# Attention, a gated product and routed experts in one kernel: order of the first attention, of g's low parts and of the router's products

## The chip, the cores and the metric

One core of a Trainium2 chip runs the whole kernel as one program. The metric is the device time in microseconds from launch to end, the median of several runs. Engines are named as the profile names them: PE (matrix products), DVE (vector), ACT (scalar), POOL (GpSimd), SP (issues nearly all DMAs).

## What is computed

```python
# _attn_ref: q, k, v are (4, 8, 576, 64); heads 0-3: a window of 32 keys, heads 4-7: every fourth key of 128
scores = np.where(masks, scale * q @ k.T, -1e9)
attn = softmax(scores)
x = attn @ v                                   # 2304 tokens x 512
# _moe_ref: d_ff = 1536
x = ((x @ w_a) * (x @ w_b)) @ w_out
# _moe2_ref: 8 experts, each token goes to the one with the largest logit
logits = (x / |x|) @ (emb / |emb|).T / tau
out[mask_e] = gate * (relu(x[mask_e] @ w1[e]) @ w2[e])
```

The weights w_a, w_b and w_out come as 64-bit floating point words and are turned into 32-bit numbers on the chip.

## The kernel before

The tokens come in four batches b = 0 to 3 of 576. Every product is made of three PE passes: a number is split into a high part (an ACT copy to a shorter format) and a low part (a subtraction on DVE or POOL), and `mm3` (lines 576 to 580) multiplies high by high, high by low and low by high. That is why lines 578, 579 and 580 carry nearly all matmuls.

**First attention** (loop at line 1019, thirteen steps). The nine row tiles j of batch 0 go through a hand-written pipeline: `scores` (PE products with the mask, DVE maxima, POOL scaling, line 434), `exp` one step later (ACT, four pieces), `norm` (POOL, DVE, POOL), `trans` (PE transposes of the weights, LAG = 3 steps after the scores), `tevac` (the copy of the transposed weights to `aT`, ACT), `av` (PE, one more step later), `oevac` (ACT writes `x0h`, DVE `x0l`). In the same steps the first two weight tiles are converted (`CONV_STEPS`), the first one is split in four quarters (`SPLIT0`, low parts on POOL), and a first part of the next products is made ahead (`PRE`). The loads are issued by SP in the order `ORDER`: mask, q/k, v, conversion words and constants.

**f loop** (line 1064; `f_step`, line 593). Each batch has twelve steps f, each over a slice of 128 columns of w_a and w_b. A step has four product groups on PE, `mm(c, hf)`: c chooses w_a or w_b, hf one half of the tokens, each into a PSUM bank of its own. After both groups of a half, `g_evac` has ACT copy one product (`a`), DVE multiply it with the other (`g`), ACT write the high part `gh` (line 610) and POOL the low part `gl` (line 611). Between the groups stand: the attention of the next batch (scores of tile f, transposes and `av` of tile f-2), `ab_split` of the next weight slice (`abh` on ACT, `abl` on DVE), and two lists of small things, `extra` after the first `g_evac` and `extra2` before the last group. In b = 0 each step also converts one weight tile (`conv_steps`: ACT scales the high words, three DVE operations assemble the number) and loads the words of a later one into one of two buffers (`conv_load`); the result is stored for the later batches. `setup2` in `extra2` of step 6 normalises the expert embeddings in a chain of small DVE operations.

**x1 stage** (`x1_run`, `x1_last`, `x1_weights`, line 662). After the twelve steps of a batch, twelve steps multiply g by w_out. In b = 0 four more tiles of w_out are converted here, one at each even step, all four parts of it ahead of the split of the next half tile (`wo_split`: `woh` on ACT, `wol` on POOL in b = 0 and on DVE later).

**Router**. The rows of x1 of a batch are multiplied with the eight expert embeddings on DVE (`logit`, line 219, one operation for each row tile and expert), during the f loop of the next batch: three in each `extra2` of b = 1 and 2, six in those of b = 3. `choose`, `rank`, `place` and the `scatter` of the rows (POOL) follow in later steps of the same generator (`steps`, line 279).

**Experts**. The rest of the time, from some 570 us on, belongs to the eight experts and is not touched.

Every engine runs its instructions in the order in which the program issues them; an instruction that waits holds up what stands behind it on the same engine. SP's DMAs too are issued in program order.

Of the kernel before, what the change touches and what calls it, by code (L numbers as in the profile page):

```python
# [29 lines left out]
LOGITS = 3  # L30
# [50 lines left out]
def fused_kernel(ctx: ExitStack, tc: tile.TileContext, qk, v, wab, wout, w1, w2, emb, tau, cst, msk, out, dbg=None):  # L81
# [51 lines left out]
    def setup():  # L133
        e_sb = cv.tile([E, DM], F32, tag="esb", name="esb", bufs=1)
        t_sb = rt.tile([E, 1], F32, tag="tsb", name="tsb", bufs=1)
        nc.sync.dma_start(out=e_sb, in_=emb)
        nc.sync.dma_start(out=t_sb, in_=tau)
        return e_sb, t_sb

    def setup2(e_sb, t_sb):  # L140
        junk = cv.tile([E, DM], BF16, tag="ejunk", name="ejunk", bufs=1)
# [37 lines left out]
    class Router:  # L179
# [208 lines left out]
    class Attn:  # L388
# [102 lines left out]
    def conv_load(i):  # L491
        if i < len(conv_src):
            t = c64[i] = cv.tile([128, 2048], I32, tag="c64", name="c64")
            nc.sync.dma_start(out=t, in_=conv_src[i].bitcast(I32))
# [11 lines left out]
    def conv_steps(i):  # L506
# [7 lines left out]
        else:  # L514
            wo_raw[i - NF] = dst
        keep = wab32[i] if i < NF else wout32[i - NF]
        words = c64[i].rearrange("p (n two) -> p n two", two=2)
        lo, hi = words[:, :, 0], words[:, :, 1]
        ou = dst.bitcast(U32)
        nc.scalar.activation(out=hi.bitcast(F32), in_=hi.bitcast(F32), func=AF.Copy, scale=REBIAS)  # L520
        yield
        nc.vector.tensor_scalar(out=ou, in0=hi.bitcast(U32), scalar1=3, scalar2=None, op0=ALU.logical_shift_left)
        yield
        nc.vector.scalar_tensor_tensor(
            out=ou, in0=hi.bitcast(U32), scalar=0x80000000, in1=ou, op0=ALU.bitwise_and, op1=ALU.bitwise_or)
        yield
        nc.vector.scalar_tensor_tensor(
            out=ou, in0=lo.bitcast(U32), scalar=29, in1=ou, op0=ALU.logical_shift_right, op1=ALU.bitwise_or)
# [63 lines left out]

    def f_step(b, f, at_cur, at_mid, at_prev, extra, extra2):
# [7 lines left out]
        def g_evac(hf, between=None):  # L601
# [6 lines left out]
            if between is not None:  # L608
                between()
# [715 lines left out]
```

## Time and profile before

| | |
|---|---|
| median of 3 runs | 825.92 us (824.6 to 826.48) |
| the profiled execution | 822.89 us, its span 821.1 us, mean granted TensorE clock 0.994 |
| busy: PE, DVE, ACT, POOL | 787.6 us (96%), 495.3 (60%), 406.1 (49%), 216.7 (26%) |
| chain that ended last, by engine | PE 56%, DVE 12%, ACT 11%, DMA 7% |
| first attention | from the start to about 35 us |
| f loop and x1 of b = 0, 1, 2, 3 | from about 35, 173, 311 and 439 us |

A busy time is that of the instructions of an engine, without what it waited for. Matmuls overlap in the array, so the duration of one (0.3 us) is longer than the distance to the next one. The releaser in square brackets behind a row is what ended the idle time before it. Records of neighbouring instructions on one engine overlap by about 0.1 us. A queue name with q (SPq) is the engine's instruction queue.

### The profile page before, as it was taken

To read this page: it belongs to the slowest core of one execution; us is meant where nothing else is said; L and a number is where in the kernel's file an instruction comes from. 1 tells how busy PE (TensorE), PEld (TensorE's weight loads), DVE (VectorE), ACT (ScalarE), POOL (GpSimd) and SP (SyncE) were. 2 spreads that over 40 slices of the span, in tenths; PEclk is the share of its full clock that TensorE was granted. 3 is DMA by queue.
4 is the path that set the end of the run, shared out by engine and by line. 5 is a ranking of instruction groups with operands and counts; after the bars stand their busy time and mean duration, and the time that the engine had idled before them with its cause. 6 is when DMAs were issued, how large, how long until landed. Compare 5 with 4: busy or idle time off the path is not lost.

```text
span 821.1 us, 15985 instructions
## 1 busy us (share of the span) xinstructions
PE 787.6 (96%) x6112; PEld 726.0 (88%) x6112; DVE 495.3 (60%) x1127; ACT 406.1 (49%) x1019; POOL 216.7 (26%) x295
## 2 busy tenths in 40 slices
PE   7899898999999999999999989999999999999995
PEld 4699897789989889998889889999889999999994
DVE  4688887737665426675645874355666555656671
ACT  6866554345654225555324244354564645745651
POOL 3544335533332203333220122341110001101111
PEclk9999999999999999999999999999999999999998
DMA  9967678699443322131143222546556546656720
GB/s 316 299 168 252 212 251 260 200 337 308 148 138 91 129 86 91 58 120 53 62 162 100 78 78 90 186 162 214 186 176 197 195 121 223 183 167 201 231 76 25
DMA packets 40293, 136.17 MB, mean 166 GB/s; under 512 B 4083, under 2 KB 4339, under 8 KB 37776
## 3 DMA queue, kind: packets, MB, share of 16 engines
q1 hardware_dynamic: 37120, 125.54, 47.3%
q0 software_dynamic: 3088, 9.52, 3.0%
q8 instruction: 50, 0.82, 0.4%
q14 instruction: 35, 0.29, 0.1%
HBM read 109.67 MB, written 25.80 MB: 165 GB/s over the span
## 4 chain that ended last, share of the span: by engine, by line
PE 56%; DVE 12%; issue 12%; ACT 11%; DMA 7%; POOL 1%; POOLq 0%; DVEq 0%; ACTq 0%
DVE jl L219 6%; PE mm L578 6%; PE mm L580 5%; PE mm L579 5%; DMA out_dram<-yo,ixi 5%; PE xr L579 4%; PE xr L580 4%; ACT s L439 4%; PE xr L578 4%; ACT abh L542 3%; PE hp L580 3%; PE hp L579 3%; PE hp L578 3%; DVE g L607 2%; PE ytp L579 2%
## 5 line engine op out<-in xcount | busy, mean ns | idle before, releaser
L578 PE MATMUL mm<-x0h,abh 128*128 128x288 f32 x768 | 235.7, 307 | 2.5 <-DVE g L607 2.5
L580 PE MATMUL mm<-x0h,abl 128*128 128x288 f32 x768 | 227.0, 296 | 1.7 <-DVE abl L543 1.7
L579 PE MATMUL mm<-x0l,abh 128*128 128x288 f32 x768 | 226.6, 295 | 0.0
L578 PEld LDWEIGHTS mm<-x0h,abh 128*128 128x128 f32 x768 | 144.4, 188 | 8.7 <-DVE g L607 3.2
L580 PEld LDWEIGHTS mm<-x0h,abl 128*128 128x128 f32 x768 | 144.5, 188 | 2.7 <-DVE abl L543 2.7
L579 PEld LDWEIGHTS mm<-x0l,abh 128*128 128x128 f32 x768 | 144.7, 188 | 0.0
L611 POOL TENSOR_TENSOR gl<-g,gh 128x288 fp32r<-128x288 f32 x96 | 85.5, 890 | 197.2 <-ACT gh L610 197.2
L610 ACT ACTIVATE gh<-g 128x288 fp32r<-128x288 f32 x96 | 42.7, 445 | 181.4 <-DVE g L607 181.4
L543 DVE TENSOR_TENSOR wl<-raw,wh 128x1024 fp32r<-128x1024 f32 x60 | 73.1, 1223 | 53.4 <-ACT wh L542 53.3
L543 DVE TENSOR_TENSOR abl<-abr,abh 128x1024 fp32r<-128x1024 f32 x47 | 57.8, 1230 | 77.4 <-ACT abh L542 77.4
L954 POOL DMA_INDIRECT out_dram<-yo,ixi x23 | 26.2, 1140 | 205.7 <-ACT yo L953 159.1
L543 DVE TENSOR_TENSOR wol<-wor,woh 128x512 fp32r<-128x512 f32 x48 | 38.5, 801 | 61.7 <-ACT woh L542 59.8
L542 ACT ACTIVATE woh<-wor 128x512 fp32r<-128x512 f32 x60 | 37.6, 629 | 74.3 <-PE xr L580 52.2
L578 PE MATMUL hp<-xTh,wh 128*128 128x352 f32 (+6 forms) x224 | 68.9, 308 | 0.0
L579 PE MATMUL hp<-xTl,wh 128*128 128x352 f32 (+6 forms) x224 | 67.7, 302 | 0.0
L580 PE MATMUL hp<-xTh,wl 128*128 128x352 f32 (+6 forms) x224 | 67.6, 302 | 0.0
L542 ACT ACTIVATE wh<-raw 128x1024 fp32r<-128x1024 f32 x64 | 67.0, 1053 | 0.0
L579 PE MATMUL xr<-wol,gh 128*128 128x512 f32 x156 | 61.4, 394 | 2.9 <-POOL wol L543 2.5
L578 PE MATMUL xr<-woh,gh 128*128 128x512 f32 x156 | 61.4, 393 | 2.3 <-ACT woh L542 1.7
L580 PE MATMUL xr<-woh,gl 128*128 128x512 f32 x156 | 60.8, 390 | 0.0
L607 DVE TENSOR_TENSOR g<-a,mm 128x288 f32<-128x288 f32 x96 | 42.6, 444 | 23.5 <-PE mm L580 19.2
L542 ACT ACTIVATE abh<-abr 128x1024 fp32r<-128x1024 f32 (+1 forms) x51 | 51.1, 1002 | 0.0
(213 smaller groups left out, 1665.7 us busy)
## 6 DMA issues: line engine op xcount, KB each, us to landing
raw<-in_w_dram SPq DMA_DIRECT2D x64, 512.0 KB, 4.5
abr<-wab SPq DMA_DIRECT2D x36, 512.0 KB, 3.9
c<-in_wab_dram SPq DMA_DIRECT2D x12, 1024.0 KB, 6.1
wor<-wout SPq DMA_DIRECT2D x24, 512.0 KB, 3.4
qkt<-in_qk_dram SPq DMA_DIRECT2D x12, 832.0 KB, 8.4
vt<-in_v_dram SPq DMA_DIRECT2D x12, 576.0 KB, 7.8
xs<-rows SPq DMA_DIRECT2D x8, 781.5 KB, 15.9
wab<-abr SPq DMA_DIRECT2D x12, 512.0 KB, 6.8
```

The lines of the kernel that those rows point to most:

```text
L219: nc.vector.scalar_tensor_tensor(out=jl, in0=rbox[0][:, self.t0 + t, :DM], scalar=1.0, in1=ebox[e // E1][:, e % E1, :], op0=ALU.mult, op1= ...
L439: nc.scalar.activation(out=self.s[:, pr, :], in_=self.src[pr], func=AF.Exp, scale=0.125, bias=self.least[:, pr:pr + 1], accum_out=self.sm[ ...
L542: nc.scalar.activation(out=hi, in_=raw, func=AF.Copy)
L543: (eng or nc.vector).tensor_tensor(out=lo, in0=raw, in1=hi.bitcast(F32), op=ALU.subtract)
L578: nc.tensor.matmul(out=out_, lhsT=lh, rhs=rh, start=first, stop=False)
L579: nc.tensor.matmul(out=out_, lhsT=lh, rhs=rl, start=False, stop=False)
L580: nc.tensor.matmul(out=out_, lhsT=ll, rhs=rh, start=False, stop=last)
L607: nc.vector.tensor_tensor(out=g, in0=a, in1=acc[1, hf], op=ALU.mult)
L610: nc.scalar.activation(out=g_hl[0][:, f, t], in_=g, func=AF.Copy)
L611: nc.gpsimd.tensor_tensor(out=g_hl[1][:, f, t], in0=g, in1=g_hl[0][:, f, t].bitcast(F32), op=ALU.subtract)
L954: nc.gpsimd.indirect_dma_start(out=out, out_offset=bass.IndirectOffsetOnAxis(ap=self.ixi[e][:m, t:t + 1], axis=0), in_=yo[:m, :], in_offse ...
```

## The change

In the first attention the transposes are issued ahead of the `av` products and LAG is 2, so that the loop has twelve steps. The load order is another: the second q/k group and a v group stand ahead of the words, the constants `c_sb` come in step 3. The conversion of the first two tiles and the quarter splits stand in later steps. The copies `aT` of the first five tiles go to DVE. In the f loop gh and gl of each half are put in a list and issued by `g_lows`: that of the second half in the next step, after the split, transposes and exp, that of the first half right after its g. The router's steps are called from `extra` and `extra2`, with two and one products in turn (b = 1 and 2) or two and two (b = 3); the x1 stage calls them twice in each step. In the x1 stage of b = 0 a conversion is spread over an even and an odd step, one word load is issued in two halves, one of them ahead into a buffer of its own, and the low parts `wol` are made by DVE. The embedding tiles use buffers of other tags.

```diff
-LOGITS = 3
-CONV_STEPS = (0, 0, 1, 1, 1, 1, 1, 1, 1, 1, 1, 0, 0, 0, 0, 0, 0, 0)
+CONV_STEPS = (0, 0, 0, 0, 1, 1, 1, 1, 0, 1, 1, 1)
 CONV1 = 3
-SPLIT0 = (6, 7, 8, 9)
-PRE = (10, 11)
-ORDER = (0, 1, 3, 1, 2, 2, 4)
-LAG = 3
+SPLIT0 = (8, 8, 9, 9)
+PRE = (9, 10)
+TEVAC_DVE = 5
+ORDER = (0, 1, 1, 2, 3, 2)
+LAG = 2
...
     def setup():
-        e_sb = cv.tile([E, DM], F32, tag="esb", name="esb", bufs=1)
+        e_sb = mp.tile([E, DM], F32, tag="wol", name="esb")
...
         def steps(self, per):
-            n = E * self.nt
-            for i in range(0, n, per):
-                for k in range(i, min(i + per, n)):
-                    self.logit(k)
+            n, i = E * self.nt, 0
+            while i < n:
+                k = min(n, i + per[0])
+                per = per[1:] + per[:1]
+                for i in range(i, k):
+                    self.logit(i)
+                i = k
                 yield
             self.choose()
-            yield
-            yield
+            for _ in range(3):
+                yield
             self.rank()
...
         def tevac(self):
             self.aT = at.tile([96, 4, 128], F32, tag="aT", name="aT")
-            nc.scalar.activation(out=self.aT, in_=self.tp, func=AF.Copy)
+            if self.early and self.j < TEVAC_DVE:
+                nc.vector.tensor_copy(out=self.aT, in_=self.tp)
+            else:
+                nc.scalar.activation(out=self.aT, in_=self.tp, func=AF.Copy)
...
+    def conv_ahead(i):
+        c64[i] = [cv.tile([128, 1024], I32, tag="c64x", name="c64x", bufs=1)]
+        nc.sync.dma_start(out=c64[i][0], in_=conv_src[i].bitcast(I32)[:, :1024])
...
-            split(wo_raw[n // 2][:, w], *hl, eng=nc.gpsimd if n < NF else nc.vector)
+            split(wo_raw[n // 2][:, w], *hl, eng=nc.vector)
...
+    g_low = []
+
+    def g_lows():
+        while g_low:
+            g_low.pop(0)()
+
...
             nc.vector.tensor_tensor(out=g, in0=a, in1=acc[1, hf], op=ALU.mult)
-            if between is not None:
-                between()
-            nc.scalar.activation(out=g_hl[0][:, f, t], in_=g, func=AF.Copy)
-            nc.gpsimd.tensor_tensor(out=g_hl[1][:, f, t], in0=g, in1=g_hl[0][:, f, t].bitcast(F32), op=ALU.subtract)
+
+            def low():
+                nc.scalar.activation(out=g_hl[0][:, f, t], in_=g, func=AF.Copy)
+                nc.gpsimd.tensor_tensor(out=g_hl[1][:, f, t], in0=g, in1=g_hl[0][:, f, t].bitcast(F32), op=ALU.subtract)
+
+            g_low.append(low)
...
             at_mid.norm()
+        g_lows()
         mm(1, 0)
         g_evac(0)
+        g_lows()
         conv(cg, 2)
...
         if b == 0:
             conv_store()
+            if i == 0:
+                conv_ahead(NF + 4)
             if i % 2 == 0:
-                conv(conv_steps(NF + 2 + i // 2))
-                conv_load(NF + 4 + i // 2)
+                x1_conv[:] = [conv_steps(NF + 2 + i // 2)]
+                conv(x1_conv[0], 2)
+            else:
+                conv(x1_conv[0], 1)
...
             wo_split(n + 1)
+        if b == 0:
+            conv(x1_conv[0], 1)
+            if i % 2:
+                conv_load(NF + 4 + i // 2)
...
+                nc.sync.dma_start(out=c_sb, in_=cst)
+            if i in (5, 9):
+                load_v()
...
-            if LAG + 1 <= i:
-                gr[i - LAG - 1].av()
             if LAG <= i < NJ + LAG:
                 gr[i - LAG].trans()
                 gr[i - LAG].tevac()
+            if LAG + 1 <= i:
+                gr[i - LAG - 1].av()
...
-                steps = router.steps(6 if last else LOGITS)
+                steps = router.steps((2, 2) if last else (2, 1))
...
                 elif router is not None:
+                    extra.append(lambda: next(steps, None))
                     extra2.append(lambda: next(steps, None))
...
-                x1_run(b, 10 if b == 0 else None, lambda i: next(steps, None))
+                x1_run(b, 10 if b == 0 else None, lambda i: [next(steps, None) for _ in range(2)])
```

## Rows read from the trace of the kernel before

**Rows 1.** Windows of 10 us: busy us (and instructions) per engine, granted clock, DMA.
```profile
20.00:30.00 10.00, 7.03 (x116) 4.85 (x113) 6.86 (x20) 9.10 (x44) 6.66 (x13) 1.00 1.00 354
160.00:170.00 10.00, 10.00 (x46) 8.28 (x45) 3.29 (x3) 2.85 (x4) 5.72 (x5) 1.00 0.68 230
460.00:470.00 10.00, 8.75 (x64) 8.19 (x63) 8.30 (x20) 2.63 (x6) 2.39 (x3) 1.00 0.31 102
```

**Rows 2.** Timeline of DVE, f loop of b = 3 (start us, us, instruction, idle before).
```profile
442.40 0.46 DVE L607 TENSOR_TENSOR g<-a,mm 128x288 f32<-128x288 f32 x1 [0.46 <-PE mm L580]
...
474.37 1.22 DVE L543 TENSOR_TENSOR abl<-abr,abh 128x1024 fp32r<-128x1024 f32 x1 [1.46 <-ACT abh L542]
...
512.88 0.45 DVE L607 TENSOR_TENSOR g<-a,mm 128x288 f32<-128x288 f32 x1
...
519.24 0.46 DVE L607 TENSOR_TENSOR g<-a,mm 128x288 f32<-128x288 f32 x1 [2.70 <-PE mm L580]
```

**Rows 3.** Timeline of ACT at three places: step 7 and x1 of b = 0; b = 3.
```profile
96.73 0.45 ACT L610 ACTIVATE gh<-g 128x288 fp32r<-128x288 f32 x1 [6.68 <-DVE g L607]
...
170.93 2.64 ACT L698 ACTIVATE rows<-xr 128x512 f32<-128x512 f32 x4 [1.76 <-PE xr L580]
...
472.95 0.44 ACT L610 ACTIVATE gh<-g 128x288 fp32r<-128x288 f32 x1 [4.48 <-DVE g L607]
```

**Rows 4.** Timeline of PE: first attention, steps 6 to 8 of b = 0, x1.
```profile
19.16 0.56 PE L413 MATMUL sc<-qkt 64*64 64x96 f32 x16 [1.72 <-DMA qkt<-in_qk_dram]
...
34.41 0.69 PE L465 MATMUL av<-aT,vt 96*64 96x64 f32 x16
...
81.82 0.34 PE L407 MATMUL sc<-mask_bf,id_bf 128*128 128x192 bf16 x2
...
90.29 0.34 PE L407 MATMUL sc<-mask_bf,id_bf 128*128 128x192 bf16 x2
...
92.74 0.60 PE L452 MATMUL atp<-ident,s 128*96 128x128 f32 x4
...
98.72 0.69 PE L465 MATMUL av<-aT,vt 96*64 96x64 f32 x16 [2.19 <-ACT aT L456]
...
101.48 0.54 PE L407 MATMUL sc<-mask_bf,id_bf 128*128 128x192 bf16 x2
...
104.97 0.60 PE L452 MATMUL atp<-ident,s 128*96 128x128 f32 x4
...
133.06 0.40 PE L578 MATMUL xr<-woh,gh 128*128 128x512 f32 x1
```

**Rows 5.** Waits of PE, 174 to 262 us (b = 1): total us, times, longest.
```profile
PE av L465 <- ACT aT L456: 1.5, 4, 0.9
```

**Rows 6.** Groups by line: x1 of b = 0, its f loop, b = 3 (busy us, mean ns).
```profile
L543 POOL TENSOR_TENSOR wol<-wor,woh 128x512 fp32r<-128x512 f32 x12 | 18.8, 1575 | 14.5 <-ACT woh L542 14.4
L527 DVE SCALAR_TENSOR_TENSOR wor<-c,wor 128x1024 uint32<-128x1024 uint32 x6 | 11.2, 1870 | 0.1
L520 ACT ACTIVATE c<-c 128x1024 f32<-128x1024 f32 x5 | 5.7, 1131 | 11.8 <-DMA c<-in_wout_dram 11.8
...
L527 DVE SCALAR_TENSOR_TENSOR abr<-c,abr 128x1024 uint32<-128x1024 uint32 x10 | 12.1, 1212 | 0.0
...
L611 POOL TENSOR_TENSOR gl<-g,gh 128x288 fp32r<-128x288 f32 x23 | 18.5, 805 | 73.7 <-ACT gh L610 73.7
L219 DVE SCALAR_TENSOR_TENSOR jl<-rows,en_a 128x512 bf16<-128x512 f32 x20 | 15.5, 777 | 0.6
```

**Rows 7.** Timeline of DVE, steps 6 (`setup2`) and 10 of b = 0.
```profile
91.90 0.67 DVE L143 SCALAR_TENSOR_TENSOR ejunk<-esb 8x512 bf16<-8x512 f32 x1
...
97.76 0.60 DVE L426 TENSOR_REDUCE amx<-sc 128x2 f32<-128x192 f32 x2
...
129.52 0.44 DVE L607 TENSOR_TENSOR g<-a,mm 128x288 f32<-128x288 f32 x1
```

**Rows 8.** The page's DMA issues: KB each, median us to landing.
```profile
c<-in_wout_dram SPq DMA_DIRECT2D x6, 1024.0 KB, 6.3
```

More of the change, by code (lines that the diff above doesn't have):

```diff
@@ L140, in setup2 @@
     def setup2(e_sb, t_sb):
-        junk = cv.tile([E, DM], BF16, tag="ejunk", name="ejunk", bufs=1)
+        junk = rt.tile([128, DM], BF16, tag="jl", name="ejunk", bufs=1)[:E, :]
         ss = rt.tile([E, 1], F32, tag="ess", name="ess", bufs=1)
@@ L492, in conv_load @@
         if i < len(conv_src):
-            t = c64[i] = cv.tile([128, 2048], I32, tag="c64", name="c64")
-            nc.sync.dma_start(out=t, in_=conv_src[i].bitcast(I32))
+            c64[i] = c64.get(i, []) + [cv.tile([128, 2048], I32, tag="c64", name="c64")]
+            w = 1024 * (len(c64[i]) - 1)
+            nc.sync.dma_start(out=c64[i][-1][:, :2048 - w], in_=conv_src[i].bitcast(I32)[:, w:])
+    def conv_ahead(i):
+        c64[i] = [cv.tile([128, 1024], I32, tag="c64x", name="c64x", bufs=1)]
+        nc.sync.dma_start(out=c64[i][0], in_=conv_src[i].bitcast(I32)[:, :1024])
     conv_kept = []
@@ L516, in conv_steps @@
         keep = wab32[i] if i < NF else wout32[i - NF]
[L517 to L520, printed above, removed]
+        parts, c = [], 0
+        for t in c64.pop(i):
+            n = min(t.shape[1] // 2, 1024 - c)
+            words = t[:, :2 * n].rearrange("p (n two) -> p n two", two=2)
+            parts.append((words[:, :, 0].bitcast(U32), words[:, :, 1].bitcast(U32), dst.bitcast(U32)[:, c:c + n]))
+            c += n
+        for lo, hi, ou in parts:
+            nc.scalar.activation(out=hi.bitcast(F32), in_=hi.bitcast(F32), func=AF.Copy, scale=REBIAS)
         yield
-        nc.vector.tensor_scalar(out=ou, in0=hi.bitcast(U32), scalar1=3, scalar2=None, op0=ALU.logical_shift_left)
+        for lo, hi, ou in parts:
+            nc.vector.tensor_scalar(out=ou, in0=hi, scalar1=3, scalar2=None, op0=ALU.logical_shift_left)
         yield
-        nc.vector.scalar_tensor_tensor(
-            out=ou, in0=hi.bitcast(U32), scalar=0x80000000, in1=ou, op0=ALU.bitwise_and, op1=ALU.bitwise_or)
+        for lo, hi, ou in parts:
+            nc.vector.scalar_tensor_tensor(out=ou, in0=hi, scalar=0x80000000, in1=ou, op0=ALU.bitwise_and, op1=ALU.bitwise_or)
         yield
-        nc.vector.scalar_tensor_tensor(
-            out=ou, in0=lo.bitcast(U32), scalar=29, in1=ou, op0=ALU.logical_shift_right, op1=ALU.bitwise_or)
+        for lo, hi, ou in parts:
+            nc.vector.scalar_tensor_tensor(out=ou, in0=lo, scalar=29, in1=ou, op0=ALU.logical_shift_right, op1=ALU.bitwise_or)
         conv_kept.append((keep, dst))
@@ L599, in mm, with g_evac @@
                 ab_mm(n, acc, c, hf, k)
-        def g_evac(hf, between=None):
+        def g_evac(hf):
             a = ap.tile([128, HALF], F32, tag="a", name="a")
@@ L689, in x1_run @@
             x1_weights(b, i, NF)
+            if i == 0:
+                g_lows()
             if i == rows_at:
@@ L711, in x1_last @@
                 x1_weights(b, j, 2 * NF)
+                if j == 0:
+                    g_lows()
                 hook(j)
@@ L1040, in fused_kernel @@
             conv(early_conv, CONV_STEPS[i])
-            if i in SPLIT0:
-                ab_split_part(0, SPLIT0.index(i))
+            for q in range(4):
+                if SPLIT0[q] == i:
+                    ab_split_part(0, q)
             if i in PRE:
```

3 lines of the change are left out of this document (1 added, 2 removed).

## The prediction

> **What bounds the kernel now.** I read the 10 us windows first. TensorE (PE) is the bound wherever it is unhindered: between 160 and 170 us it runs 46 matmuls, so one takes 0.217 us. Three stretches of another kind stand beside it [rows 1]: the first attention (20 to 30 us), where PE is busy 7.03 of 10 us, ACT 9.10 and DMA all of the time; the f loop of b=3 (460 to 470 us), where PE has 8.75 and DVE 8.30 with DMA at 0.31; and, further down, the x1 stage of b=0. The gain can come from such stretches alone, so I next asked each what PE waits for. In b=3 the first g of the batch starts at 442.40, the last but one pair stands at 512.88 and 519.24 [rows 2]. The last pair is a step that only PE bounds: 6.36 us. Eleven of them are 69.96 us, and 442.40 to 519.24 is 76.84. So 6.9 us are lost there. The engine that shows why is ACT: it sits 4.48 us before gh, released by DVE's g [rows 3]. DVE works off six router products between the two g of a step, the g of the second half waits behind them, gh waits for that g, and because ACT runs in order the next split (abh) waits behind gh; abl on DVE in turn waits for abh [rows 2, 3]. The same link is seen in b=0: ACT waits 6.68 us for g and so comes late to the aT copy, and PE's av products wait 2.19 us [rows 3, 4]; and in b=1 the waits of av on aT make 1.5 us [rows 5] (the same row, 1.5 us, stands for b=2).
>
> **The change part by part.** Its own time is that of the profiled execution, 822.89 us (span 821.1 plus 1.8 around it); the median of the runs is 825.92, 3.0 higher. I sum savings and take them off the median.
>
> (1) g's low part (gh on ACT, gl on POOL) of the second half is issued one step later, behind the next abh, aT and exp; that of the first half stays right behind its g. Nothing is added: as many instructions, in another order. What is now queued behind gh on ACT is only a of the next first half, and gl's reader is the x1 stage, up to 11 steps away. So the link "g to next abh and aT" is cut.
>
> (2) b=3: four products a step instead of six, two on either side of the third product group, in eight steps instead of five and a bit. DVE per step then: 4 x (0.78 for the product + 0.08 read, an estimate from the pitch) + 1.23 for abl + 2 x 0.46 for g = 5.6 us [rows 2, 6], under PE's 6.36. Before: 6 x 0.86 + 1.23 + 0.92 = 7.3, and the wait for abh on top. The choice and rank of tokens move later (f=8 and 9 instead of 6 and 8), and the four row scatters on POOL follow in f=10 and 11, no later than the last stood before; the rank's few matmuls stay. Of the 6.9 us I keep 0.4 for those: **6.5** (5.5 to 6.9).
>
> (3) b=1 and b=2: still three products a step, but two before and one after av, and aT no longer behind gh. The waits of rows 5 go, twice 1.5: **2.9** (2.0 to 3.2). Choosing in f=11 of b=1 now precedes the last g; PE needs that bank only after three further row tiles of x1, 9 x 0.217 = 1.95 us on, so I cost it at nothing; without that cover it costs the choice, seven small DVE operations at some 0.2 us (4.2 us for 21 in rows 7, see (4)): 1.5.
>
> (4) b=0, step 7. The chain of 21 small DVE operations for the embedding norm starts at 91.90, and DVE reaches the next maxima at 97.76 [rows 7]; less the g (0.45) and the conversion (1.21, rows 6) between, the chain is 4.2 us. PE's score products start at 81.82, 90.29 and 101.48: 8.47 for the step before, 11.19 for this one, so 2.7 us lost. [...] With the link cut aT is early. What is late next is the score bank: the next scores need this step's exp, exp needs the maxima, and DVE starts those only at 97.76. They take 0.60; POOL's scaling and exp's four pieces have no row here, I put them at 1.5 (1.0 to 2.1). That gives 99.9 instead of 101.48, 1.6 gained (1.0 to 2.1), and with a wait that short I take it that the clock stays: 1.04 more. **2.7** (1.0 to 3.8, the upper end if DVE, no longer chained through ACT, is ahead when the chain begins).
>
> (5) x1 of b=0. The first product starts at 133.06, and the first evacuation, at 170.93, waits for the last product of its row tile [rows 3, 4]. Unhindered that is 11 steps of 12 matmuls plus 3 more and a tail of 0.3: 135 x 0.217 + 0.3 = 29.6 us. It took 37.9, so 8.3 are lost. ACT waits 11.8 us there for the loaded words, and POOL's low parts take 1.58 each [rows 6]. The change splits the four conversions over even and odd steps, puts half of one load ahead, and moves the 12 low parts to DVE. That adds DVE 0.7 each (half as wide as abl, whose 1.23 is in rows 2; bounds 0.6 and 1.2), two per 5.2 us pair, and takes it from POOL. The last conversion operation took 1.87 mean here and 1.21 in the f loop [rows 6]; if POOL's absence brings it back, a pair needs 3.5 + 1.4 = 4.9 us of DVE, just under PE's 5.2, with waits of up to 1 us left at each odd step. Walking through by these prices I get 1.3 us if the words arrive as before. But the word load behind the first wait is issued when DVE has finished the conversion two tiles before, and DVE there is late through the link that (1) cuts: step 10 ends on PE at about 133.06 - 6.36 = 126.7, its last g starts at 129.52 [rows 4, 7], 2.8 later; the load itself takes 6.3 [rows 8]. So the first pair comes 2 to 3 us sooner. **3.2** (0.5 to 5.5).
>
> (6) The first attention. Loads are reordered so that the second q/k group comes before the converted words; the lag falls from 3 to 2, so the loop has 12 steps for 13, and transposes go ahead of the av products. The seventh tile's scores start at 19.16 on the third q/k load and the last av at 34.41 [rows 4]: 15.25 us, six steps, 2.54 each. As many bytes stand ahead of that load as before (but for the small constants), so 19 us stays; from there five steps remain. That would give 2.5. Against it: ACT is the pace (9.10 of 10), it keeps its exp, copies, one word scaling and now all four quarter splits in two steps; only the aT copies of five tiles go to DVE, most of them before 19 us, where the load hides them. Also the second conversion ends after the loop, and the split of f=1 waits for it. At the worst nothing is gained, at the best the five steps also run 0.2 us faster each, 3.5: **2.0** (0 to 3.5).
>
> Moving the embedding tiles to other buffers and c_sb to a later place: they wait for nothing that is near; nothing.
>
> Sum 6.5 + 2.9 + 2.7 + 3.2 + 2.0 = 17.3; 825.92 - 17.3 = **808.6** (a profiled span near 804).
>
> [...] POOL's gl takes 0.81 us in b=3 [rows 6], and now the second half's gl runs beside abl. [...]
>
> **The rivals.**
> (A) As forecast, 808.6.
> (B) The conversion sets b=0's pace: terms 4 to 6 are used up by word loads that land late. For it: DMA is full in the attention [rows 1], and the conversion of the second tile now ends later there, with the load of the fourth behind it. Against: a load has 6.3 us in an 8.47 us step. Left are 6.5 + 2.9: 816.5.
> [...]
> (D) The new attention opens a PE wait like the 2.19 us of rows 4 (the early products need the first quarter splits, which come two steps later), and the clock falls: 1.04 to 1.7 us, 810. Before, a wait at 19.16 left the clock at full. [...]
> (E) Slower: two word buffers. A word tile is held about 9.5 us (estimate: a step of 8.47 and 1 more, from its scaling at a step's start to the last operation after its end), two steps are 16.9; so a load above 7.4 us stretches each step by half the excess. At 6.3 it doesn't; at 9.4, which the denser start would have to bring, 1.0 x 14 steps = 14 us are lost on top of terms 4 to 6: 831. It decides from 7.4 on, and outweighs 9.4 us of sure gain from about 8.8.
>
> **How the numbers follow.** A 0.66, B 0.13, C 0.10, D 0.07, E 0.04. A's own ends are 816.9 (9.0 in all) and 803.0 (22.9) if all terms are low or high together, which is not likely. The range 803.5 to 815.5 holds A, C and D and leaves out B and E (0.17). A measurement of this kernel can tell about 0.2% (1.7 us). All but E lie far below it; allowing for an error in a term I have not seen: faster 0.93, same 0.03, slower 0.04.
>
> **What would show it.** Right: g pitch of 6.36 to 6.4 in all of b=3 and no ACT idle before abh; av waits on aT gone in b=1 and b=2; scores of steps 7 and 8 of b=0 under 10 us apart, clock 1.00; 46 matmuls per 10 us in more of x1; the last av before 33 us. Wrong: a DVE busy share above 0.95 in b=3 (C), ACT waiting on words in the f loop (B, E), a granted clock under 1 in the attention (D).

## The result, and the profile after

The changed kernel takes 816.9 us (median of 4 runs, 814.9 to 819.4) beside 826.2 us of the kernel before (4 runs): a ratio of 0.990, 95% interval 0.987 to 0.993. It is faster by 9.3 us, not by 17.3: the forecast was 808.6, and the time lies 1.4 us above the upper end of its range, 815.5. The profiled execution's span went from 821.1 to 813.1 us, its mean granted clock from 0.994 to 0.988.

To see where the time went I cut both spans at the same instructions. The third column is the kernel of the first experiment below (old first attention, all the rest changed); the last is the change that the forecast's terms gave to the stage.

| stage, us | before | after | old attention | forecast |
|---|---|---|---|---|
| start to first scores of the f loop | 35.29 | 37.55 | 35.38 | -2.0 |
| first to third scores | 12.88 | 14.25 | 12.86 | 0 |
| third to seventh scores | 33.92 | 33.91 | 33.92 | 0 |
| seventh to ninth scores (step 7) | 19.87 | 20.57 | 18.78 | -1.7 |
| ninth scores to x1 of b=0 | 31.10 | 32.18 | 31.72 | -1.0 |
| x1 of b=0 to its first evacuation | 37.87 | 35.47 | 36.28 | -3.2 |
| to the first scores of b=2 (b=1) | 138.58 | 136.75 | 136.77 | -1.45 |
| to the first g of b=3 (b=2) | 132.89 | 130.03 | 130.04 | -1.45 |
| to the last g but one pair (b=3) | 76.84 | 70.18 | 70.19 | -6.5 |
| the rest, mostly experts | 301.86 | 302.21 | 302.06 | 0 |

Term (4), 2.7, has two places in this table: 1.66 in step 7, and 1.04 behind the ninth scores. b=1 to b=3 gave 11.4 us, more than the 9.4 that were forecast. b=0 as a whole became longer: 170.9 us before, 173.9 after.

Windows of 10 us after (columns as in [rows 1]):
```profile
20.00:30.00 10.00, 6.15 (x107) 4.07 (x99) 8.42 (x23) 7.33 (x37) 3.96 (x10) 1.00 0.78 237
30.00:40.00 10.00, 9.24 (x102) 7.73 (x102) 4.19 (x12) 6.37 (x19) 4.54 (x7) 0.83 0.62 214
...
100.00:110.00 10.00, 7.10 (x60) 6.00 (x59) 8.45 (x20) 4.77 (x16) 3.25 (x5) 0.70 0.48 156
...
460.00:470.00 10.00, 10.00 (x78) 10.00 (x77) 8.77 (x21) 4.52 (x8) 2.84 (x3) 1.00 0.27 98
```
The last row is the success: in b=3 PE is busy all the time (8.75 before). The first is the failure: between 20 and 30 us PE is busy less than before (6.15 for 7.03), ACT too (7.33 for 9.10), and DMA is at 0.78 instead of 1.00; then, at 30 to 40 and 100 to 110, the granted clock is down (0.83 and 0.70, where the kernel before had 1.00 and 0.83).

DVE, POOL and ACT in b=3 (timelines: start us, us, instruction, idle before):
```profile
440.71 0.46 DVE L629 TENSOR_TENSOR g<-a,mm 128x288 f32<-128x288 f32 x1 [0.46 <-PE mm L596]
441.08 0.69 DVE L219 SCALAR_TENSOR_TENSOR jl<-rows,en_a 128x512 bf16<-128x512 f32 x1
...
441.81 1.27 DVE L219 SCALAR_TENSOR_TENSOR jl<-rows,en_a 128x512 bf16<-128x512 f32 x1
...
510.89 0.46 DVE L629 TENSOR_TENSOR g<-a,mm 128x288 f32<-128x288 f32 x1 [2.70 <-PE mm L596]
```
```profile
441.73 0.80 POOL L633 TENSOR_TENSOR gl<-g,gh 128x288 fp32r<-128x288 f32 x1 [19.75 <-ACT gh L632]
445.48 1.24 POOL L633 TENSOR_TENSOR gl<-g,gh 128x288 fp32r<-128x288 f32 x1 [2.95 <-ACT gh L632]
```
```profile
456.39 1.06 ACT L558 ACTIVATE abh<-abr 128x1024 fp32r<-128x1024 f32 x1 [0.99 <-PE mm L595]
...
460.28 0.45 ACT L632 ACTIVATE gh<-g 128x288 fp32r<-128x288 f32 x1 [1.70 <-DVE g L629]
```
From the first row to the g at 510.89 it is 70.18 us, eleven steps of 6.38. What ends ACT's idle ahead of abh is now PE giving back the buffer (nine times in b=3, 1.2 us at most), not gh's wait for g (4.48 in [rows 3]). DVE and POOL run beside one another twice in a step: a product beside gl takes 1.27 us instead of 0.69, and a gl beside abl 1.24 instead of 0.80. With DVE at 8.77 and PE at 10.00 of 10 us this costs nothing here.

### The profile page after: what moved, and what is told of

Same layout as the page of the kernel before. It is cut to its first block, busy times and chain, and to the rows that moved or that the text cites. A ratio compares the mean times of both kernels' runs of the same rounds, so it can differ in the third digit from the quotient of the medians.

```text
span 813.1 us, 16000 instructions
## 1 busy us (share of the span) xinstructions
PE 787.5 (97%) x6112; PEld 729.0 (90%) x6112; DVE 519.6 (64%) x1147; ACT 411.6 (51%) x1015; POOL 218.8 (27%) x283
## 4 chain that ended last, share of the span: by engine, by line
PE 73%; DMA 8%; issue 7%; DVE 5%; ACT 3%; POOL 1%; SPq 0%; POOLq 0%; DVEq 0%; ACTq 0%
PE mm L594 11%; PE mm L596 10%; PE mm L595 10%; DMA out_dram<-yo,ixi 5%; PE xr L595 4%; PE xr L594 4%; PE xr L596 4%; PE hp L595 3%; PE hp L596 3%; PE hp L594 3%; PE av L471 2%; PE ytp L595 2%; PE ytp L596 2%; PE ytp L594 2%; PE atp L455 2%
## 5 line engine op out<-in xcount | busy, mean ns | idle before, releaser
L633 POOL TENSOR_TENSOR gl<-g,gh 128x288 fp32r<-128x288 f32 x96 | 95.1, 996 | 114.0 <-ACT gh L632 114.0
L559 DVE TENSOR_TENSOR wol<-wor,woh 128x512 fp32r<-128x512 f32 x60 | 46.3, 772 | 67.6 <-ACT woh L558 63.1
L558 ACT ACTIVATE woh<-wor 128x512 fp32r<-128x512 f32 x60 | 37.8, 630 | 78.5 <-PE xr L596 56.7
L632 ACT ACTIVATE gh<-g 128x288 fp32r<-128x288 f32 x96 | 42.4, 442 | 65.8 <-DVE g L629 65.8
L437 POOL TENSOR_SCALAR least<-amx 128x4 f32<-128x4 f32 x36 | 23.4, 650 | 152.4 <-DVE amx L434 100.6
```

The costliest lines, as they stand in the source:

```text
L437: nc.gpsimd.tensor_scalar(out=self.least, in0=mx, scalar1=0.125, scalar2=None, op0=ALU.mult)
L558: nc.scalar.activation(out=hi, in_=raw, func=AF.Copy)
L559: (eng or nc.vector).tensor_tensor(out=lo, in0=raw, in1=hi.bitcast(F32), op=ALU.subtract)
L632: nc.scalar.activation(out=g_hl[0][:, f, t], in_=g, func=AF.Copy)
L633: nc.gpsimd.tensor_tensor(out=g_hl[1][:, f, t], in0=g, in1=g_hl[0][:, f, t].bitcast(F32), op=ALU.subtract)
```

## What went wrong in the first attention

**Undo that part alone.** Theory: the new attention is a loss, not a gain of 2.0.
```diff
-CONV_STEPS = (0, 0, 0, 0, 1, 1, 1, 1, 0, 1, 1, 1)
-SPLIT0 = (8, 8, 9, 9); PRE = (9, 10); TEVAC_DVE = 5; ORDER = (0, 1, 1, 2, 3, 2); LAG = 2
+CONV_STEPS = (0, 0, 1, 1, 1, 1, 1, 1, 1, 1, 1, 0, 0)
+SPLIT0 = (6, 7, 8, 9); PRE = (10, 11); TEVAC_DVE = 0; ORDER = (0, 1, 3, 1, 2, 2, 4); LAG = 3
 # and av ahead of trans, c_sb ahead of the loop, the second v group one step later
```


> The changed kernel with the first attention of the kernel before (lag 3, av ahead of the transposes, old load order, old places of the conversion, all aT copies on ACT); all else as changed. Theory A: the new first attention itself loses time: the scores of step f=0 came 2.3 us later than before and those of f=2 3.6 us later. With the old one the f=0 scores stand at 35.0 and those of f=2 at 48.2 us again, and the whole gains 3.6 against the changed kernel: span 809.5, about 813. Rival B: the word loads of the f loop set the pace of b=0 anyway, and the x1 stage starts no earlier than 138 us: within 1 us of the changed kernel.

Measured: 810.1 us (809.7 to 810.9), ratio 0.982 (0.978 to 0.985). That is 6.7 us under the whole change and even under the 813 of the theory; the table's third column shows that b=0 lost less afterwards, too. So the new first attention costs 6.7 us (7.2 by the two ratios), and the rest of the change alone gains 14.8, where the other terms of the forecast sum to 15.3.

**Why.** The waits of PE from the start to 45 us (total us, times, longest), after, and then with the old attention:
```profile
PE atp L455 <- POOL s L450: 6.6, 8, 1.9
```
```profile
PE sc L410 <- ACT s L442: 2.3, 2, 1.2
PE av L471 <- ACT aT L462: 2.0, 2, 1.0
PE sc L416 <- DMA qkt<-in_qk_dram: 1.5, 2, 1.0
```
The transposes of the softmax weights wait for POOL's product s in eight steps. One such step on PE, DVE and POOL, kernel after (timelines as above):
```profile
25.52 0.56 PE L416 MATMUL sc<-qkt 64*64 64x96 f32 x16
27.27 0.64 PE L455 MATMUL atp<-ident,s 128*96 128x128 f32 x4 [1.20 <-POOL s L450]
...
30.76 0.64 PE L455 MATMUL atp<-ident,s 128*96 128x128 f32 x4 [1.91 <-POOL s L450]
```
```profile
23.29 1.58 DVE L541 SCALAR_TENSOR_TENSOR abr<-c,abr 128x1024 uint32<-128x1024 uint32 x1
24.79 0.61 DVE L429 TENSOR_REDUCE amx<-sc 128x2 f32<-128x192 f32 x2
26.13 0.18 DVE L449 RECIPROCAL asm<-asm 128x4 f32<-128x4 f32 x1 [0.73 <-POOL asm L448]
```
```profile
25.56 0.23 POOL L437 TENSOR_SCALAR least<-amx 128x4 f32<-128x4 f32 x1 [1.77 <-DVE amx L429]
25.87 0.23 POOL L448 TENSOR_SCALAR asm<-asm 128x4 f32<-128x4 f32 x1
26.39 0.83 POOL L450 TENSOR_TENSOR s<-s,asm 128x384 f32<-128x384 f32 x1 [0.30 <-DVE asm L449]
```
Read from the end: the transposes at 27.27 wait for s, which ends at 27.22; s for the reciprocal; the reciprocal for POOL's asm; asm, which belongs to an older tile, stands on POOL behind `least` of the newer one; `least` waits for the maxima, and those stand on DVE behind a conversion operation of 1.58 us. With a lag of two the transposes of a tile come one step after its s was issued, so this whole queue lies between one step's scores and the next step's transposes, and the next scores stand on PE behind those. This step takes 3.5 us (27.27 to 30.76) where [rows 4] gave 2.54. With a lag of three a further step lies between. The seventh tile's scores and the last av of the kernel after:
```profile
19.55 0.56 PE L416 MATMUL sc<-qkt 64*64 64x96 f32 x16
...
36.66 0.69 PE L471 MATMUL av<-aT,vt 96*64 96x64 f32 x16
```
The first came when it was forecast (19 us); the five steps from there took 17.1 us, 3.42 each, partly at a granted clock of 0.50 (from 32.3 to 35.7 us). The other traces agree: in all six kernels with a lag of two PE waits 5.5 to 8.8 us for s, and these five steps take 17.1 to 18.2 us. In the fourteen with a lag of three there is no such wait but one of 1.4, and the six steps take 15.3 to 17.0 us, except in two (18.9 and 21.1).

**Which part.** Six more kernels mix the two attentions; all else is as changed. "Loop" is the lag, the transposes ahead of the products and the copies on DVE; "places" are the loads, the conversion steps, the quarter splits and the early products.

| loop | places | first, third scores at | time, us |
|---|---|---|---|
| old | old | 35.4, 48.2 | 810.1 |
| new, but lag 3 | old | 38.1, 51.0 | 811.1 (810.4 to 814.4) |
| new | old | 41.6, 54.7 | 818.2 (817.4 to 819.1) |
| old | old, new loads | 42.4, 55.3 | 815.3 (814.5 to 818.6) |
| old | new | 41.4, 55.9 | 820.1 (819.0 to 822.1) |
| new, but lag 3 | new | 37.1, 51.8 | 814.0 (813.3 to 816.5) |
| new | new, old loads | 39.1, 53.9 | 817.6 (817.1 to 817.9) |
| new | new (the change) | 37.6, 51.8 | 816.9 (814.9 to 819.4) |

Their edits are the lines of the diff above, taken singly. In the order of the rows two to seven:

> The kernel with the old first attention (810.14), with only the transposes put ahead of the products and the five aT copies on VectorE; the lag stays three, loads and places as before. Theory N (the lag of two closes the loop of one step): TensorE waits under 1 us for GpSimd's product, the first scores of b=0 start at 34.5 to 36, the time is 809 to 811. Theory V (the order, or the copies on VectorE ahead of the reciprocals, slow it whatever the lag): the first scores start at 37 us or later, the time is 812 to 818.

> The kernel with the old first attention (810.14) with only its loop changed: lag of two, transposes ahead of the products, five aT copies on VectorE; loads, conversion steps, quarter splits and early products stay where they were before. Theory N (the loop of one step costs the attention, the moved conversion and splits cost the two steps after it): TensorE waits 4 us or more for GpSimd's product, the first scores of b=0 start at 36.5 to 37.5, the first to the third scores take 12.9 us as in the old attention (14.3 in the changed kernel), the time is 811 to 813. Theory P (the moved conversion and splits make both losses): the first scores start at 35.5 or sooner, one step fewer even gives 34, the time is 808.5 to 810.5.

> The kernel with the old first attention (810.14), with only the loads in their new order (second q/k group ahead of the converted words, the constants in the loop, v one step sooner); the conversion keeps its steps, from the third on. Theory L (the later words stop VectorE and ScalarE, whose conversion steps now stand ahead of their data): ScalarE waits 2 us or more for the words in the attention, the first scores start at 37 or later, the time is 812 to 818. Theory P (the late conversion and the splits crowded into two steps cost, not the loads): the first scores within 1 us of 35.4, the time is 809.5 to 811.

> The opposite: the loop of the first attention as before (lag of three, products ahead of the transposes, aT on ScalarE), with the new order of the loads and the new places of the conversion, the quarter splits and the early products. Theory N: no wait for GpSimd's product, the first scores of b=0 start at 35.3 to 36.3, but the first to the third scores take 14 us or more since the second conversion ends 7 us later, the time is 811.5 to 813.5. Theory P: the first scores start at 37 or later, the time is 814 to 817. If neither loss is here (35.5 and 12.9), the loss comes only from both together, 810.

> The changed kernel with the lag of the first attention set back from two steps to three (13 steps again); the transposes stay ahead of the products, the loads, the copies on VectorE and the split places stay as changed. Theory N (the loop of one step): with a lag of two, a tile's aT copy, the next reciprocal, GpSimd's product s and the next transposes follow each other inside every step, and TensorE waits for s 6.6 us in all; with a lag of three the product has a step of slack, so that wait falls under 1.5 us, the first scores of b=0 start near 36 us (37.55 in the changed kernel, 35.29 before), and the time is 812 to 815. Theory L (the loads): the place of the loads and of the second conversion sets the end, the first scores stay at 37.5 or later, the third set of scores at 51.8 or later, and the time is 816 to 819.

> The changed kernel with the loads of the first attention in their order of before (the converted words ahead of the second q/k group, the small constants ahead of the loop, the second v group at the seventh step); its loop with a lag of two stays. Theory N (the loop of one step): TensorE's wait for GpSimd's product stays at 5 us or more, the first scores of b=0 start at 37 us or later, the time is 815 to 819. Theory L (the loads): the second conversion ends near 34 us again (40.9 in the changed kernel), the first scores start near 35.5, the third set near 48.5, and the time is 810 to 812.

What follows. The lag of two costs 7.0 us in the old places (818.2 against 811.1) and 2.8 in the new ones (816.9 against 814.0; there the ranges overlap, and the two profiled executions, 814.9 and 816.5, stand the other way round), and with it PE's wait for s comes and goes:
```profile
PE atp L455 <- POOL s L450: 8.8, 8, 2.1
```
```profile
PE atp L455 <- POOL s L450: 1.4, 1, 1.4
```
(the new loop in the old places with a lag of two, then of three; waits of PE to 55 us). Transposes ahead and copies on DVE cost 1.0 us at most, which can't be told from nothing. The new order of the loads costs 5.2 us by itself: the words come later, ACT waits 5.46 us for them with exp queued behind, and PE waits 6.01 us for exp (ACT, then PE, in that kernel; its profiled execution was the slowest of the four, 818.6 us):
```profile
16.00 1.10 ACT L535 ACTIVATE c<-c 128x1024 f32<-128x1024 f32 x1 [5.46 <-DMA c<-in_wab_dram]
```
```profile
18.12 0.64 PE L410 MATMUL sc<-mask_bf,id_bf 128*128 128x192 bf16 x2 [6.01 <-ACT s L442]
```
The later conversion steps of the change avoid that wait, but then the second conversion ends at 41.0 us instead of before the loop, and f=1's abh and the word load behind it come late (ACT, kernel after):
```profile
41.02 1.06 ACT L558 ACTIVATE abh<-abr 128x1024 fp32r<-128x1024 f32 x1 [2.11 <-DVE abr L544]
...
48.21 1.15 ACT L535 ACTIVATE c<-c 128x1024 f32<-128x1024 f32 x1 [3.08 <-DMA c<-in_wab_dram]
```
This is the 1.4 us between first and third scores: 14.3 to 14.8 in the four kernels with new places, 12.9 to 13.2 in the four with old ones. Along the rows one, two, six and eight of the table the 6.7 us are 1.0 for the order and the copies, 2.9 for the new places and 2.8 for the lag. Of my prices for the halves (1 to 3 us each) none held: each half alone costs 8 to 10 us, both together 6.7. They don't add up. Each alone lets the clock fall further than both together (0.83 in this stretch); that this makes the difference is likely, not shown. Windows of the new loop alone, then of the new places alone:
```profile
30.00:40.00 10.00, 7.11 (x64) 5.95 (x66) 4.77 (x11) 4.37 (x19) 5.44 (x6) 0.60 0.76 242
```
```profile
30.00:40.00 10.00, 7.42 (x51) 5.42 (x51) 2.73 (x11) 4.80 (x19) 4.69 (x8) 0.66 0.62 217
```
Why the new places alone cost most of all stays open; one wait that the change does not have is PE's of 1.1 us for POOL's part of a quarter split.

A mark comes from one execution, and it wanders: the nine kernels here with the very same old attention began their first scores at 35.1 to 40.4 us. In rows two, four and six the profiled execution was the slowest of its four by 2 to 3 us, in row eight it was the fastest. And the kernel before, run beside each group of kernels, had medians from 824.6 to 826.2. The verdicts above go by the times, and differences of 1 or 2 us between two marks are not read.

## b=3: two cuts, one would do

> The changed kernel, but the low parts of both halves are issued right after their g in every batch; the router's products stay spread. Theory A: b=1 and b=2 owe their gain to the deferral and lose it (4 to 5 us), and in b=3 the chain g, gh, abh, abl, g, four products makes 6.7 us a step for PE's 6.36, another 2 to 3 us; b=0 gains 1 to 2: 822. Rival B: the spread alone does it, in all batches: within 2 us of the changed kernel.

> The changed kernel with the router's products where they were before (three, in b=3 six, in one place ahead of the last product group, one call in each x1 step); the low parts stay deferred. Theory A: in b=3 DVE has 7.3 us of work in a step of 6.36, so the first steps run at 7.3: some 5 us of that batch's 6.7 are lost again, b=1 and b=2 keep their gain: 822. Rival B: the wait of the split behind gh was the whole cause, the deferral alone brings 6.36 us steps: within 1 us of the changed kernel.


```diff
         g_evac(1)
+        g_lows()          # first kernel: no deferral, products spread as changed
...
-                steps = router.steps((2, 2) if last else (2, 1))   # second: deferral, products as before
+                steps = router.steps((6,) if last else (3,))   # and called once a step
```
Measured: 820.6 and 818.8 us (ratios 0.995 and 0.993), but little of what they lose to the change lies in b=3: their f loops begin 1.7 and 1.3 us later, and the first takes 2.2 us more in x1 of b=0. By stage, b=3 takes 70.83 without the deferral and 70.44 without the spreading, beside 70.18 with both and 76.84 with neither. So either cut alone opens the loop: without the six products in a row g is early enough for gh, and with gh deferred a late g holds up nobody (without the spreading gh still waits up to 3.7 us for g, but abh for PE alone). My shares in b=3 (2 to 3 us for the deferral, some 5 for the spreading) were wrong: taking one away cost 0.65 or 0.26, since the other does its work. In b=1 and b=2 the deferral is worth about 0.8 us each (137.5 and 130.95 without it), the spreading next to nothing (136.8 and 130.2 without it); without the deferral 1.1 and 1.9 us of the gain stay.

## b=0: step 7 and x1

**Step 7.** The kernel after, timelines of ACT and of PE:
```profile
103.63 1.06 ACT L558 ACTIVATE abh<-abr 128x1024 fp32r<-128x1024 f32 x1 [5.45 <-DVE abr L544]
```
```profile
102.51 0.40 PE L594 MATMUL mm<-x0h,abh 128*128 128x288 f32 x1 [1.75 <-DVE g L629]
105.70 0.64 PE L410 MATMUL sc<-mask_bf,id_bf 128*128 128x192 bf16 x2 [1.15 <-ACT s L442]
```
The deferral moved gh behind abh and exp. But in b=0 abh waits for the last conversion operation (line 544), which stands on DVE behind that same g. The link that I called cut is there a second time. PE waits 1.75 and 1.15 us, and the clock is at 0.50 from 104 to 110.7 us.

> The first attention of before and everything else as changed, but in b=0 g's second low part is issued at once. It stands against the kernel with the old first attention, 810.14. Theory A (as in the forecast, the deferral pays in b=0 too): the seventh to the ninth scores lie 20 us apart instead of 18.78, x1 begins over 1 us later, 811.5 to 812.5. Theory B (abh waits in b=0 for the last operation of the conversion, which stands behind that same g, so the deferral frees nothing there): every mark within 0.4 us, the time 809.7 to 810.6, and the 2.3 us that the same edit cost the changed kernel was the spread of the new first attention.

> The first attention of before and everything else as changed, but the chain of 21 small VectorE operations for the embedding norm, in one step of b=0 so far, is given out over six steps. It stands against the kernel with the old first attention, 810.14. Theory A (the chain is the cause of the late step): the seventh to the ninth scores take 16.9 to 17.3 us instead of 18.78, the time is 807.5 to 808.7. Theory B (VectorE has no room): it holds 7.8 us of work in a step of 8.47, 0.7 more a step fills it, six steps become 0.2 to 0.4 us longer, and the time is 809.5 to 811.


```diff
         g_evac(1)
+        if b == 0:
+            g_lows()                                   # first kernel
...
-                if b == 0 and f == 6:                  # second kernel
-                    extra2.append(lambda: es.append(setup2(*es[0])))
+                if b == 0 and f == 4:
+                    es_steps = setup2(*es[0])          # now a generator, some operations a step
+                if b == 0 and 4 <= f < 10:
+                    extra2.append(lambda: next(es_steps, None))
```
The same undoing in the changed kernel with its new attention had given 819.2 us, with the first scores at 40.7:

> The changed kernel, but in b=0 alone the low parts of the second half are issued right after their g, as before. Theory A: in b=0 the next split waits on ACT for the last conversion operation, which stands behind g on DVE, so that the deferral cut nothing there; it only put gh between exp and the next a, and two gl side by side beside the conversion. Then the distance of the scores of f=6 and f=8 falls from 20.6 us to 19.9 or less and x1 starts some 1.8 us earlier: 815. Rival B: the deferral does shorten the way to the conversion of the last tiles, and x1 loses 1 to 2 us without it: 818.

Measured: 812.9 us without the deferral in b=0 (810.1 with it). 1.2 of the 2.8 us lie in the start of that execution, 0.4 in step 7, 1.1 in x1. So it frees little where I looked for it. The time is far from theory B's (809.7 to 810.6) and 0.4 above theory A's, but the place that A named is not it: the seventh to the ninth scores take 19.2 us, not 20. With the chain spread the seventh to the ninth scores take 16.96 us, two steps of 8.48: the chain was the whole loss of step 7, and DVE has room for it. Yet the time is 811.8, not lower: x1 took 37.8 instead of 36.3, and the stage ahead of it 0.6 more.

**x1.** With the old attention, PE and ACT:
```profile
138.50 0.50 PE L594 MATMUL xr<-woh,gh 128*128 128x512 f32 x1 [1.67 <-ACT woh L558]
```
```profile
130.10 1.15 ACT L535 ACTIVATE c<-c 128x1024 f32<-128x1024 f32 x1 [3.15 <-DMA c<-in_wout_dram]
136.80 1.14 ACT L535 ACTIVATE c<-c 128x1024 f32<-128x1024 f32 x1 [3.09 <-DMA c<-in_wout_dram]
143.40 1.14 ACT L535 ACTIVATE c<-c 128x1024 f32<-128x1024 f32 x1 [4.09 <-DMA c<-in_wout_dram]
```
woh stands on ACT behind a scaling whose words have not landed; after that wait the clock is at 0.83 between 140 and 150 us. Two theories: the order on ACT and DVE, or the words, which come every 6.6 us, where PE needs a new pair every 5.44 us (24 matmuls, 0.68 us for three).

> The kernel with the old first attention (810.14), and in x1 of b=0 the split of the next weight tile is issued ahead of the scaling of the loaded words in the even steps (it was behind it). Theory S (ScalarE's order: woh stands behind words that have not landed, TensorE waits 1.7 us at the second step and its clock falls to half): no wait of TensorE for woh, clock 1.00 in x1, first x1 product to first evacuation 32 to 33.5 us instead of 36.2, the time is 806.5 to 808. Theory W (the words themselves set the pace of x1): the wait moves to the next tile of the converted weights, the stage stays at 35.5 us or more, the time is 809.5 to 811.

> As the run before it, and the embedding-norm chain is given out over six steps. Alone the chain's 1.8 us were given back in x1. Theory S: with the split ahead, x1 no longer takes them, the time is 1.3 to 2 us under the run before it, 805 to 806.5. Theory W: x1 ends when the words have come, so nothing is added: within 0.5 us of the run before it.

> The kernel with the old first attention (810.14), and in x1 of b=0 every split of the next weight tile is issued ahead of the conversion steps, even and odd. Theory S2 (the order on ScalarE and VectorE sets x1): TensorE waits under 0.7 us for woh and wol in all, the clock stays at 1.00, first x1 product to first evacuation 31.5 to 33 us instead of 36.2, the time is 805.5 to 807.5. Theory W (the words set x1's end): the scaling of the words still comes every 6.6 us, the waits move to the tiles of the next pair, 35 us or more, the time is 809 to 811.

> As the run before it, and the embedding-norm chain is given out over six steps. Theory S2: x1 starts 1.3 us sooner and keeps at least half of that at its end: 804 to 806.5, at least 0.6 under the run before it. Theory W: x1's end stands where the words put it, the time is within 0.5 us of the run before it.

> The kernel with the old first attention, splits ahead and the chain spread (808.69), and in b=0 the half tile of words that is loaded ahead is that of the fourth output weight tile, a load issued two f steps before x1, instead of that of the fifth. Theory W (the words set x1's end): the scaling of the fourth tile, 7.4 us behind the third's so far, comes 4.5 to 6 us behind it, the wait of TensorE for wol at 149.0 (1.1 us) goes or moves to the fifth tile, x1 takes 34 to 35.2 us instead of 35.8, the time is 807 to 808.5. Theory E (the engines' order sets it): x1 within 0.3 us of 35.8, the time within 0.5 us of 808.7.


```diff
         if b == 0:
             conv_store()
+            if i + 1 < n_i:
+                wo_split(n + 1)              # split_all; split_first only for even i
...
+            if f == 9:                       # words_ahead: in f_step, instead of conv_ahead(NF + 4) in x1
+                conv_ahead(NF + 3)
             conv_load(n + 4)
```

| with the old attention | x1, us | time, us |
|---|---|---|
| alone | 36.3 | 810.1 (809.7 to 810.9) |
| even splits ahead | 35.9 | 810.4 (809.5 to 812.3) |
| even splits ahead, chain spread | 37.4 | 810.1 (809.3 to 812.8) |
| all splits ahead | 36.0 | 810.4 (808.1 to 812.8) |
| all splits ahead, chain spread | 35.8 | 808.7 (807.3 to 809.8) |
| the same, words of the fourth tile ahead | 35.3 | 812.9 (811.4 to 816.1) |

With all splits ahead the wait for woh is gone and the clock holds (ACT and a window of that kernel):
```profile
131.91 1.17 ACT L535 ACTIVATE c<-c 128x1024 f32<-128x1024 f32 x1 [2.38 <-DMA c<-in_wout_dram]
139.55 1.13 ACT L535 ACTIVATE c<-c 128x1024 f32<-128x1024 f32 x1 [3.37 <-DMA c<-in_wout_dram]
147.02 1.11 ACT L535 ACTIVATE c<-c 128x1024 f32<-128x1024 f32 x1 [3.48 <-DMA c<-in_wout_dram]
```
```profile
140.00:150.00 10.00, 8.74 (x36) 6.61 (x36) 6.60 (x8) 4.42 (x7) 0.99 (x1) 1.00 0.98 341
```
But x1 is no shorter: the words now come every 7.6 and 7.5 us, PE's waits have moved to wol (3.0 us in three), and all its waits in x1 grew from 3.0 to 3.7 us. So the order theory falls, and the words are the likelier bound: a load starts when DVE has freed one of two buffers (the kernel after has SP waiting 19.3 us for it there, in four waits), and DMA is at 0.98. The run meant to settle it met neither forecast. With half a tile's words ahead ACT waits for none after 142 us, but the loads behind are later: ACT waits 5.38 us for words just ahead of x1, PE 2.70 for ACT at its start, and then the clock is at 0.67 from 145 to 150. x1 fell by 0.5, but the stage ahead of it rose by 2.8 (from 32.3 to 35.1), and the whole by 4.2 (in the profiled execution the first scores, too, came late, at 40.4). The wait for words was moved, not taken away; whether buffers or bandwidth make it stays open. A third whole buffer, which would tell, was not tried.

The kernel with all splits ahead and the chain spread is the fastest seen: ratio 0.979 (0.977 to 0.981), 8.2 us under the change. Its lead over the old attention alone, 1.4 us, is not clear of the spread: the two intervals overlap.

**The low parts wol.**

> The kernel with the old first attention (810.14), and the 12 low parts of x1's weights in b=0 are made by GpSimd as before. By the forecast (GpSimd's part takes 1.58 us each and slows the conversion's last operation on VectorE from 1.21 to 1.87): x1 takes 37 to 37.9 us instead of 36.2, the time is 811 to 812. Rival (words set x1's end, so who makes the low parts doesn't matter): x1 36.0 to 36.5 us, the time is 809.7 to 810.6.


```diff
-            split(wo_raw[n // 2][:, w], *hl, eng=nc.vector)
+            split(wo_raw[n // 2][:, w], *hl, eng=nc.gpsimd if n < NF else nc.vector)
```
Measured: 812.7 us (812.3 to 813.1), x1 38.7 instead of 36.3. Groups by line in x1 (busy us, mean ns), wol on DVE and then on POOL:
```profile
L559 DVE TENSOR_TENSOR wol<-wor,woh 128x512 fp32r<-128x512 f32 x11 | 7.6, 687 | 5.6 <-ACT woh L558 5.6
L541 DVE SCALAR_TENSOR_TENSOR wor<-c,wor 128x1024 uint32<-128x1024 uint32 x4 | 6.0, 1494 | 0.0
L544 DVE SCALAR_TENSOR_TENSOR wor<-c,wor 128x1024 uint32<-128x1024 uint32 x4 | 4.9, 1222 | 0.1
```
```profile
L559 POOL TENSOR_TENSOR wol<-wor,woh 128x512 fp32r<-128x512 f32 x11 | 17.9, 1629 | 14.8 <-ACT woh L558 14.8
L541 DVE SCALAR_TENSOR_TENSOR wor<-c,wor 128x1024 uint32<-128x1024 uint32 x4 | 8.3, 2072 | 0.1
L544 DVE SCALAR_TENSOR_TENSOR wor<-c,wor 128x1024 uint32<-128x1024 uint32 x4 | 5.6, 1401 | 0.1
```
The move to DVE is worth 2.6 us in time and 2.4 in the stage, as much as the change gained there: the subtraction itself takes 0.69 for 1.63 us, and the conversion beside it 1.49 and 1.22 for 2.07 and 1.40.

## Why the prediction was wrong, step by step

- **(6), the first attention, is the step that failed.** I counted five steps of 2.54 us for six, "at the best" each 0.2 us faster, and asked only whether loads or ACT could use that up; the worst case was a gain of 0. What I left out: the way of a tile from its scores to its transposes (maxima, POOL's scaling, exp, sums, reciprocal, POOL's product) through queues in which other work stands ahead of it (above, 1.58 us of conversion on DVE). A lag of two leaves a step less for it, and it did not fit: the seventh tile took 7.7 us from its scores to its transposes (19.55 to 27.27), where two steps of 2.54 are 5.1. So the five steps took 3.42 us each, 17.1 in all and not 12.7. Instead of -2.0 the stage gave +2.3 (a single mark, which wanders) and the f steps behind it +1.4; in time, 6.7 us, of which the lag makes 2.8 (in the old places it makes 7.0), the new places 2.9. Rival D named the consequence (a PE wait, then a low clock), at 1.0 to 1.7 us and for another reason (the quarter splits; a wait for these, 0.6 and 1.1 us, came only with the new places and a lag of three). In the trace after, PE is busy 6.15 of 10 us from 20 to 30 us, and from 30 to 40 the granted clock is 0.83.
- **"The second conversion ends after the loop, and the split of f=1 waits for it" stood in (6), without a price.** It was 1.4 us.
- **(4), step 7: 2.7 forecast, 1.66 in the step and 1.04 behind it; losses of 0.7 and 1.1 came.** "With the link cut aT is early" was not followed to abh, which waits for a conversion operation behind the same g. With the old attention this stage gains 1.1 and the next gives 0.6 back, less than the low end of 1.0. Why the same code takes 1.8 us more in step 7 behind the new attention, no run shows. Nor does a run show that the 1.04 hangs on the length of PE's wait: with the old attention and no deferral in b=0, PE waits 2.19 us for aT, as before, and the transposes come 2.45 us behind the scores (3.49 before); with the deferral it waits 1.34 us for exp, and they come 3.26 behind; with the chain spread, no wait, 2.45.
- **(5), x1: 3.2 forecast, 2.4 came** (1.6 with the old attention). The unhindered length was too short: I took 0.217 us a matmul, from 46 in 10 us; their distance is 0.2268 (kernel after, 150 to 170 us), so 135 are 30.9 us with the tail, and 7.0 us were lost before, not 8.3. The words, rival B's mechanism, probably hold what is left of x1. That B's 816.5 is 0.4 from the measured time is luck: x1 gained 2.4, term 6 was a loss and not nothing, and b=1 to b=3 gave 2.0 more than B left them.
- **(2) b=3 was right:** 6.66 for 6.5, DVE 5.58 us a step (8.77 of 10 by 6.36) for 5.6. The reason given was half of it.
- **(3) b=1 and b=2: 4.7 for 2.9.** The waits of PE for aT are gone, as said; 1.8 and 2.9 us were gained where the waits view listed 1.5 each. For the rest I have no row.
- (E) did not come; of the terms (6) was a loss, and in this kernel (4) too. The sum without term 6 was 15.3, and 14.8 was measured, with (3) too small against (4) and (5) too large.

## What to carry to other kernels

Before a software pipeline's lag is shortened, add up the way of one item through every engine in its order of issue, with what stands ahead on each, and compare it with the step: the count of steps saved is the small part. When an operation is deferred to free what stands behind it, look for a second way by which the same operation still holds it up. A gain in one stage can be lost in the next: the 1.8 us that the spread chain gave in step 7 came back in the two stages behind it. With all splits of x1 ahead the same move took 1.7 us off the median (810.4 to 808.7), though the ranges overlap.

## What the runs showed of the hardware

PE waits of 1.75 and 1.15 us, 3.2 apart (step 7 after), and of 2.06 and 1.38, 3.1 apart (new loop in old places), went with 6.7 and 10.2 us at a granted clock of 0.50; four waits of 0.7 to 1.2 us in x1 with all splits ahead, the clock at 1.00 throughout, went with none. The two slow-downs of the first attention together cost 6.7 us, less than either alone (8.0 and 9.9). And the same first attention took from 35.1 to 40.4 us in nine executions; its DMA share was 1.00 to 1.03 from 5 to 30 us in the two with the even splits ahead (first scores at 36.4 and 35.1).
